# Agent attention and soft MoE on one core: the last product with its slots normalised ahead and its output written transposed

## The chip, the core and the metric

One core of one Trainium2 chip. The metric is the device time of one execution in microseconds, the median of several runs. The engines are TensorE (PE, with its weight loads PEld), VectorE (DVE), ScalarE (ACT), GpSimd (POOL) and SyncE (SP), which issues nearly all transfers here.

## The reference

Two layers in a row, all in float32. The first is an attention through 49 agents per batch, the second a mixture of experts over 32 slots:

```python
a2k = sm(agents, k)                 # (4, 49, 11456)
agent_v = a2k @ v                   # (4, 49, 128)
q2a = sm(q, agents)                 # (4, 11456, 49)
x = (q2a @ agent_v).reshape(45824, 128)

logits = x @ phi                    # (45824, 32 slots)
d = softmax(logits, over tokens)
slot_input = d.T @ x                # 32 x 128, four slots for each of 8 experts
slot_out[e] = relu(slot_input[e] @ w1[e]) @ w2[e]
c = exp(logits - logits.max(1))     # softmax over the slots
c /= c.sum(1) + 1e-9
return c @ slot_out                 # (45824, 128)
```

The softmax over tokens needs every token's logits before the experts can run, and the last product needs the experts' slot outputs.

## The kernel before

A cell is 128 tokens: 32 from each of four streams of a batch. A batch has 90 cells, the four batches 360. Cells are handled in groups of 16 (the last of a batch has 10). For each group of keys the kernel makes scores, a running maximum, exponentials, transposes and the weighted sum of v; for each group of queries it makes scores, the softmax over the agents, the logits of the slots (`lt`), their maximum per slot for the rounds of the token softmax, and their maximum per token.

The main part is written out as steps in one list, `ORDER`. A step's name is a family with an index (`qs.0`, `ke.1`), and steps of one family follow each other in the order of their groups. Each engine runs its own steps in list order. `BUFS` gives the number of buffers of each kind of tile.

The steps that matter here are those of the combine weights c. `cr` (DVE, L551) takes the row maximum `rm` of a group's logits, `cu` (POOL, L555) subtracts it into a buffer `xc`, `ce` (ACT, L561) takes the exponential, and `ct` (DVE, L565) transposes 32x32 blocks of it into `c_all`, the weights of all cells with the slots on partitions. For one group (`CT_PE`) the transpose is made by PE and ACT (`cp`, `cq`). The weights are left unnormalised.

The end of the list holds the last rounds of the token softmax (`r1` to `r5` for the maxima; `ru`, `re`, `rm`, `rg` for dt, its exponential, its product with `rt` and the sum on PE), then the merging of the rounds into the slot inputs `si`, the reciprocal `dr` of the token sums, the experts (`mh`, `mr` with tile `hs`, `mt` with tile `htp`, `mc` with tile `ht`, `mo`), their copies `so` and the product `sb`, which repeats the 32 slot outputs over four groups of 32 partitions. `fl` are matmuls without use, which keep PE running.

Then comes the output stage. Four cells make a quad, 90 quads in all. `c_split` (DVE L1043, POOL L1044) splits six quads of `c_all` into a high and a low part in a reduced float32 format (fp32r). `bd_hi` (L1058) and `bd_lo` (L1062) are the same for the slot outputs times `dr`, as block-diagonal matrices of two blocks, each block with a column of ones for the row sums. For a quad, PE makes three products (high by high, low by high, high by low) for two halves: six matmuls of 258 columns (L1079). DVE adds EPS to the row sums and takes the reciprocals (L1086, L1088); for each pair of quads DVE evicts the first with the reciprocals multiplied in (L1099), ACT the second in four pieces (L1103). Outputs go out in 17 batches of one to three pairs, with two transfers each, tokens on partitions.

Of the kernel before, what the change touches and what calls it, by code (L numbers as in the profile page):

```python
# [16 lines left out]
S = E * SE  # L17
P = 128
# [4 lines left out]
NQUAD = B * NCELL // 4  # L23
FULL = NCELL // 4 * 4
# [25 lines left out]
qx qx qs.0 qs.1 qx qt.0 qs.0 qt.1 qm kx qs.1 qE.0 qt.0 qE.1 qs.0 qt.1 kv qm qs.1 qE.2 qt.0  # L50
qp.0 qu ks.0 qE.3 qt.1 ks.1 kx qm qe qp.1 km.0 qc.0 qp.0 qw@0 km.1 qc.1 qp.1 qc.0 qr kt qw@1
qE.0 kv kr qr ks.0 qE.1 kb ks.1 km.0 kn ke.0 kx qp.0 km.1 ke.1 kP.0 qE.2 kt kr kb kT.0 kn ka
kP.1 kx qE.3 ks.0 kT.1 ke.0 ks.1 km.0 ke.1 kT.0 qp.1 kv qc.1 km.1 qw@2 qc.0 kE kT.1 qc.1 qr kx
kt ks.0 kA kr kb kE km.0 kn ka ke.0 ke.1 kT.0 kv kT.1 ks.1 kA ks.0 km.1 kt kE km.0 kx kr kb kv
ks.1 kA kn ka ke.0 km.1 ke.1 ks.0 kT.0 kt ks.1 kr kT.1 kx kb kn km.0 ka kE ke.0 km.1 ke.1 kT.0
kT.1 kt kv kr kE kA qx kb ks.0 kA kn ka ke.0 ks.1 ke.1 km.0 kT.0 km.1 kv kT.1 kt qs.0 kr kb kE
qt.0 kn ke.0 kx ke.1 kT.0 qs.1 kA kT.1 kg.2 qt.1 kg.1 kE kh.1 kh.2 qm kh.4 kv qu kg.3 kA ks.0
kh.3 ks.1 km.0 qe qx ql.0 km.1 ql.1 qn.0 kt ql.0 qn.1 kr qg ql.1 qn.0 kb kx qp.0 qn.1 kn ka qM
qp.1 ke.0 qg qs.0 cr ke.1 qM cu qc.0 qs.1 qt.0 qc.1 ql.0 ce r1 kv qt.1 ql.1 qn.0 qm ks.0 kT.0
r2 qE.0 ks.1 km.0 qx ql.0 kT.1 qE.1 km.1 ql.1 qn.0 r3 kx qE.2 ct kE cr qw@3 cu qE.3 kt qs.0 kA  # L60
kr ce qx qp.0 qt.0 rx kb qs.1 ct qc.0 kn ks.0 qr ka qt.1 ke.0 qn.1 qm r4 ke.1 qg qp.1 kT.0 r5
# [36 lines left out]
qu qc.1 ql.1 qn.0 r5 ru.0 qe cr ql.0 w1 qn.1 ql.1 ru.1 re.0 qn.0 ql.0 qM rm.0 re.1 qn.1 ql.1
rm.1 r1 qM w2 r2 rg.0 cu r3 qn.0 rx rg.1 r4 cr rc qp.0 ce qn.1 qp.0 r5 cu qc.0 en@12 cr qc.0
qp.1 w2 ru.0 qM ce qp.1 ql.0 qc.1 en@13 r1 en@14 qc.1 r2 ru.1 re.0 ql.1 qn.0 r3 ql.0 qn.1 rx  # L100
rm.0 re.1 w2 en@19 r4 qM ql.1 r5 fl rm.1 rg.0 qn.0 fl r1 cr ru.0 r2 rg.1 cr fl rc qn.1 fl w1
ru.1 en@15 re.0 r3 qM rx cr en@16 r4 rm.0 re.1 r1 ct en@17 r5 ct en@18 r2 fl rm.1 rg.0 r3 nm
rx wt fl ru.0 r4 f0 rg.1 r5 wr fl rc ws fl ru.0 re.0 f1 fl f2 fl rm.0 fl cu re.0 fl fl rm.0
rg.0 cu ce rg.0 rc gl fl cu fl l0 ce ct gm l1 fl cp l2 d0 cu ce l3 d1 l4 fl ct d2 mh ct ce ct
mh mr mh mr mt mt mc mr mh mc mt mr mo mc mt zz mo mc mo ms mo sb ms fl sb fl fl fl fl fl fl
fl
"""
BUFS = {
    "kt": 2, "vt": 3, "qt": 3, "es": 1, "et": 2, "pt": 8, "pT": 3, "lt": 5, "xc": 3, "dt": 2,
    "s": 4, "a": 3, "m": 1, "hs": 2, "ht": 3,  # L110
}
SUB_DVE = ()
MUL_DVE = (11, 12)
CT_PE = (21,)
# [1089 lines left out]
```

## Time and profile before

| | |
|---|---|
| median of 3 runs | 343.92 us (343.78 to 346.8) |
| the profiled execution | 343.8 us, its span as well; nothing lies around it |
| PE, DVE, ACT, POOL busy | 306.9, 283.7, 216.8, 145.6 us |
| read from and written to HBM | 79.98 MB, 23.59 MB |
| keys and queries up to the last maxima | 0 to about 244 us |
| last rounds, slot inputs, experts | 244 to 267.6 us |
| output stage | 267.66 us to the end |

A row of a view has the start or a count, the busy time, the engine, the line of the kernel and the tiles written and read; the time in brackets is how long the engine stood idle before it, with what ended that. Busy time of an engine in an average over the span says little here, since the three stretches differ; the rows by stretch and the chain of work that ended last are to be read together.

### The profile page before, as it was taken

The numbers are of one execution on the slowest core, as the hardware profiler recorded it, in microseconds if no ns is written. First come the engines' busy times: TensorE is split into PE (matmuls) and PEld (weight loads), VectorE is DVE, ScalarE is ACT, GpSimd is POOL, SyncE is SP. The second block draws the span as 40 slices with busy tenths as digits, with TensorE's granted clock in tenths as the row PEclk, the third lists the DMA queues.
The fourth block names the chain that finished last, engine by engine and source line by source line (L and its number), as shares of the span: only waits on it lengthen the run. The fifth ranks groups of instructions, "written<-read, shape, count | busy, mean of one in ns | idle before, by whom it ended". The sixth has DMA issues, their size and how long they took to land.

```text
span 343.8 us, 10606 instructions
## 1 busy us (share of the span) xinstructions
PE 306.9 (89%) x4177; PEld 207.9 (60%) x4177; DVE 283.7 (83%) x686; ACT 216.8 (63%) x773; POOL 145.6 (42%) x157
## 2 busy tenths in 40 slices
PE   2979979988988988898999999998989999999991
PEld 0235446554553554445655646487756999999990
DVE  0855755999999899999999999999894788888872
ACT  1597323494968586668776984555442577777772
POOL 0100001319371636447147937797955133444400
PEclk9999998999999999999999999999999999999996
DMA  7999899999889369989659961998000278888887
GB/s 302 423 407 363 287 409 425 418 396 379 334 322 369 126 225 418 352 309 382 270 218 396 378 272 19 394 421 350 2 2 4 92 286 357 359 342 343 336 348 295
DMA packets 16897, 104.25 MB, mean 303 GB/s; under 512 B 2000, under 2 KB 2128, under 8 KB 8144
## 3 DMA queue, kind: packets, MB, share of 16 engines
q1 hardware_dynamic: 16416, 102.95, 75.3%
q8 instruction: 33, 0.54, 0.6%
q10 hardware_dynamic: 432, 0.63, 0.5%
q14 instruction: 16, 0.13, 0.1%
HBM read 79.98 MB, written 23.59 MB: 301 GB/s over the span
## 4 chain that ended last, share of the span: by engine, by line
PE 42%; DVE 40%; ACT 6%; DMA 5%; issue 2%; POOL 1%; SPq 0%; ACTq 0%; DVEq 0%; POOLq 0%
PE po L1079 19%; DVE pt L444 6%; DVE cm L546 5%; PE sk L241 5%; PE ev L329 4%; DVE mx L449 4%; DVE et L311 4%; DVE kmx L273 3%; ACT pt L470 3%; DVE rm L551 3%; PE sq L241 3%; DMA qt<-qT 3%; DMA cs<-cst 3%; DVE row L285 3%; DVE lt L500 2%
## 5 line engine op out<-in xcount | busy, mean ns | idle before, releaser
L1103 ACT ACTIVATE ot<-po,rc 128x128 f32<-128x128 f32 x180 | 51.3, 368 | 19.3 <-DVE rc L1088 18.5
L470 ACT ACTIVATE pt<-pt,mx 128x49 f32<-128x49 f32 x160 | 51.4, 328 | 10.4 <-DVE mx L449 10.3
L241 PE MATMUL sq<-qt,ag 128*32 128x512 f32 (+1 forms) x384 | 48.0, 597 | 7.8 <-ACT ag L170 6.7
L329 PE MATMUL ev<-vt,et 128*64 128x129 f32 x720 | 46.4, 280 | 4.1 <-issue 1.4
L241 PE MATMUL sk<-kt,ag 128*32 128x512 f32 (+1 forms) x384 | 46.9, 573 | 1.4 <-DVE pt L444 1.0
L329 PEld LDWEIGHTS ev<-vt,et 128*64 128x64 f32 x720 | 40.2, 138 | 11.6 <-issue 4.9
L1044 POOL TENSOR_TENSOR cl<-c_all,ch 128x768 fp32r<-128x768 f32 x15 | 28.1, 1876 | 44.7 <-DVE rc L1086 38.6
L454 POOL TENSOR_TENSOR pt<-pt,mx 128x784 f32<-128x784 f32 (+1 forms) x14 | 19.3, 1378 | 57.2 <-DVE mx L449 56.3
L1079 PE MATMUL po<-bd_hi,ch 128*128 128x258 f32 x180 | 38.4, 295 | 0.2
L273 DVE TENSOR_REDUCE kmx<-sk 128x1 f32<-128x512 f32 (+1 forms) x48 | 30.6, 638 | 8.2 <-PE sk L241 7.9
L555 POOL TENSOR_TENSOR xc<-lt,rm 128x512 f32<-128x512 f32 (+1 forms) x24 | 24.5, 1024 | 28.4 <-DVE rm L551 22.9
L1079 PE MATMUL po<-bd_lo,ch 128*128 128x258 f32 x180 | 36.3, 283 | 0.0
L1079 PE MATMUL po<-bd_hi,cl 128*128 128x258 f32 x180 | 36.2, 282 | 0.0
L444 DVE STREAM_TRANSPOSE pt<-sq 128x512 f32<-128x512 f32 (+1 forms) x48 | 31.2, 659 | 2.2 <-PE sq L241 1.9
L1099 DVE TENSOR_TENSOR ot<-po,rc 128x512 f32<-128x512 f32 x45 | 31.1, 691 | 1.7 <-DVE rc L1088 0.2
L681 POOL TENSOR_TENSOR dt<-lt,mb 128x512 f32<-128x512 f32 (+1 forms) x24 | 28.6, 1209 | 8.1 <-ACT mb L675 7.4
L521 ACT COPY pT<-tp 128x512 f32<-128x512 f32 (+1 forms) x48 | 25.3, 556 | 9.9 <-PE tp L514 9.6
L311 DVE STREAM_TRANSPOSE et<-es 128x512 f32<-128x512 f32 (+1 forms) x46 | 29.8, 650 | 1.5 <-ACT es L300 1.5
L470 ACT ACTIVATION_READ_ACCUMULATOR pt<-pt,mx 128x1 f32 x160 | 30.6, 191 | 0.0
L300 ACT ACTIVATE es<-sk,nm 128x512 f32<-128x512 f32 (+1 forms) x48 | 29.3, 649 | 0.2
L505 POOL TENSOR_TENSOR lt<-lt,rt 128x512 f32<-128x512 f32 (+1 forms) x19 | 19.0, 999 | 23.4 <-DVE lt L500 23.3
L1079 PEld LDWEIGHTS po<-bd_hi,ch 128*128 128x128 f32 x180 | 27.6, 189 | 2.2 <-ACT bd_hi L1058 0.4
(134 smaller groups left out, 570.1 us busy)
## 6 DMA issues: line engine op xcount, KB each, us to landing
vt<-vL SPq DMA_DIRECT2D x20, 1032.0 KB, 9.5
qt<-qT SPq DMA_DIRECT2D x20, 1024.0 KB, 8.3
kt<-kT SPq DMA_DIRECT2D x20, 1024.0 KB, 7.0
out<-ot SPq DMA_DIRECT2D x26, 768.0 KB, 4.8
w1s<-w SPq DMA_DIRECT2D x4, 1024.0 KB, 9.9
w2s<-w SPq DMA_DIRECT2D x4, 1024.0 KB, 11.3
vt<-vL SPq DMA_DIRECT2D x4, 645.0 KB, 8.3
kt<-kT SPq DMA_DIRECT2D x4, 640.0 KB, 7.4
```

The lines of the kernel that those rows point to most:

```text
L241: t_.matmul(sp[32 * q4:32 * q4 + 32, :nt], ag[:, b, 32 * h:32 * h + 32], xv[:, q4, :], start=True, stop=True)
L273: v_.tensor_reduce(out=k["mx"][:, h:h + 1], in_=k["s"][h][:, :nt], axis=AX.X, op=ALU.max)
L300: s_.activation(out=k["e"][:, h, :nt], in_=k["s"][h][:, :nt], func=AF.Exp, bias=k["nm"][:, h:h + 1])
L311: v_.transpose(out=k["et"][:, :n, 32 * h:32 * h + 32], in_=k["e"][:, h, :nt].rearrange("p (t a) -> p t a", a=32))
L329: t_.matmul(k["ev"][o:o + 64, :], k["et"][:, c, :], k["v"][:, c, :], start=c < 2, stop=c >= n - 2)
L444: v_.transpose(out=q["pt"][:, :n, 32 * h:32 * h + 32], in_=q["s"][h][:, :nt].rearrange("p (t a) -> p t a", a=32))
L470: s_.activation(out=x, in_=x, func=AF.Exp, bias=q["mx"][:, c:c + 1], accum_out=q["dn"][:, c:c + 1])
L681: eng.tensor_tensor(out=q["dt"][:, :n], in0=q["lt"][:, :n, :], op=ALU.subtract, in1=r["mb"].unsqueeze(1).to_broadcast([P, n, S]))
L1044: nc.gpsimd.tensor_tensor(out=cl[:, :n], in0=src, in1=ch[:, :n].bitcast(F32), op=ALU.subtract)
L1079: t_.matmul(po[:, hf, 0:2 * VC], lh[:, i, :], rh[hf], start=ti == 0, stop=ti == 2)
L1099: v_.tensor_tensor(out=ov[0], in0=pos[2 * j][:, :, :, 0:C], in1=rc[:, 0].unsqueeze(3).to_broadcast([P, 2, 2, C]), op=ALU.mult)
L1103: s_.activation(out=ov[1][:, ha, hb], in_=pos[2 * j + 1][:, ha, hb, 0:C], func=AF.Copy, scale=rc[:, 1, ha, hb:hb + 1])
```

## The change

The combine weights now stay with the tokens on partitions: `cu` and `ce` write straight into `x_all`, which takes the place of `c_all`, and `xc`, `ct`, `cp`, `cq` and `c_split` are gone. The 360 cells are cut into 24 chunks (8, 21 times 16, 8, 8). For each chunk DVE takes the row sums, adds EPS and takes the reciprocals (`o_sum`, step `os`), POOL multiplies the weights by them (`o_mul`, step `om`), and DVE transposes the chunk into one of four `ct` buffers (`o_tr`, step `ot`). Six chunks are summed and multiplied, and four transposed, inside the list ahead of the output stage; the others inside the stage's loop, three chunks and one chunk ahead.

In the product the roles of the operands change: the slot outputs times `dr` (`sob`, one ACT activation, step `sd`) are the stationary operand and the weights the moving one, in plain float32. The 32 slots of each of the four streams stand in their own 32 partitions, so a chunk takes four matmuls with 32 contraction rows each, on four different row groups of PE, into four banks of PSUM. The result has the 128 channels on partitions. DVE copies one bank, ACT three, with no scaling, and one transfer takes the chunk out; the host puts the transposed output into its place.

```diff
-CT_PE = (21,)
-CG = 6
-OUT_SIZES = [1, 2] + [3] * 13 + [2, 1]
+CHUNKS = [8] + [16] * 21 + [8, 8]
+C0 = [sum(CHUNKS[:j]) for j in range(len(CHUNKS))]
+NORM = 6
+EARLY = 4
...
         def cu():
-            q["xc"] = tile_("xc", [P, QC, S], f"xc_{i}")
-            nc.gpsimd.tensor_tensor(out=q["xc"][:, :n, :], in0=q["lt"][:, :n, :],
+            nc.gpsimd.tensor_tensor(out=x_all[:, at:at + n], in0=q["lt"][:, :n, :],
...
-        def ct():
-            for c, m, o_ in c_spans(b, g):
-                v_.transpose(out=c_all[:, o_ * S:(o_ + m) * S],
-                             in_=q["xc"][:, c:c + m, :].rearrange("p c s -> p (c s)"))
...
+    def m_dr():
+        s_.activation(out=z["sob"], in_=z["sb"], func=AF.Copy, scale=dr)
+
+    def o_sum(j):
+        x = x_all[:, C0[j]:C0[j] + CHUNKS[j]]
+        z["cd", j] = wl(f"cd_{j}", [P, CHUNKS[j]], tag="cd", bufs=NORM)
+        v_.tensor_reduce(out=z["cd", j], in_=x, axis=AX.X, op=ALU.add)
+        v_.tensor_scalar(out=z["cd", j], in0=z["cd", j], scalar1=EPS, scalar2=None, op0=ALU.add)
+        v_.reciprocal(out=z["cd", j], in_=z["cd", j])
+
+    def o_mul(j):
+        n = CHUNKS[j]
+        x = x_all[:, C0[j]:C0[j] + n]
+        nc.gpsimd.tensor_tensor(out=x, in0=x, op=ALU.mult,
+                                in1=z["cd", j].unsqueeze(2).to_broadcast([P, n, S]))
+
+    def o_tr(j):
+        n = CHUNKS[j]
+        z["ct", j] = z["ct"][j % BUFS["ct"]]
+        v_.transpose(out=z["ct", j][:, :n * S],
+                     in_=x_all[:, C0[j]:C0[j] + n].rearrange("p c s -> p (c s)"))
...
-        for ti, (lh, rh) in enumerate([(ch, bd_hi), (cl, bd_hi), (ch, bd_lo)]):
-            for hf in range(2):
-                t_.matmul(po[:, hf, 0:2 * VC], lh[:, i, :], rh[hf],
-                          start=ti == 0, stop=ti == 2)
...
+    op_ = ctx.enter_context(tc.tile_pool(name="op", bufs=4, reuse_waits="tile"))
+    psO = ctx.enter_context(tc.tile_pool(name="psO", bufs=2, space=PSUM, reuse_waits="tile"))
...
+        for j, n in enumerate(CHUNKS):
+            if NORM <= j + 3 < len(CHUNKS):
+                o_sum(j + 3)
+                o_mul(j + 3)
+            if EARLY <= j + 1 < len(CHUNKS):
+                o_tr(j + 1)
+            po = psO.tile([P, 4, 512], F32, name=f"po_{j}", tag="o")
+            for r in range(4):
+                t_.matmul(po[:, r, :32 * n], z["sob"][32 * r:32 * r + 32, :],
+                          z["ct", j][32 * r:32 * r + 32, :32 * n], start=True, stop=True)
+            ot = op_.tile([P, 4 * 512], F32, name=f"ot_{j}", tag="ot")
+            ov = ot[:, :128 * n].rearrange("p (r x) -> p r x", r=4)
+            v_.tensor_copy(out=ov[:, 0], in_=po[:, 0, :32 * n])
+            s_.copy(out=ov[:, 1:4], in_=po[:, 1:4, :32 * n])
+            nc.sync.dma_start(out=out[:, 128 * C0[j]:128 * (C0[j] + n)], in_=ot[:, :128 * n])
```

In the list `ORDER` every `ct` is left out and `os`, `om`, `ot` and `sd` are put in near its end; the other steps keep their order. Three places show what that does on an engine. In the rows, a line number is that of the kernel the row belongs to, the tile written stands left of the arrow, and the shape is partitions by columns.

DVE where the last maxima of the queries are done (`rm` and `m_all`). Before:

```order
L551 TENSOR_REDUCE rm_3742<-lt_3680 128x10
L565 STREAM_TRANSPOSE c_all<-xc_3544 128x512
L565 STREAM_TRANSPOSE c_all<-xc_3585 128x512
L663 TENSOR_REDUCE m_all<-t_12_3758 32x1
L780 TENSOR_REDUCE nmx<-m_all 32x1
```

After:

```order
L541 TENSOR_REDUCE rm_3694<-lt_3632 128x10
L875 TENSOR_REDUCE cd_3701<-x_all 128x8
L876 TENSOR_SCALAR cd_3701<-cd_3701 128x8
L877 RECIPROCAL cd_3701<-cd_3701 128x8
L875 TENSOR_REDUCE cd_3712<-x_all 128x16
L876 TENSOR_SCALAR cd_3712<-cd_3712 128x16
L877 RECIPROCAL cd_3712<-cd_3712 128x16
L622 TENSOR_REDUCE m_all<-t_12_3718 32x1
L732 TENSOR_REDUCE nmx<-m_all 32x1
```

Two transposes gave their place to the row sums of the first two chunks.

POOL at the same time, among the last rounds' dt tiles (L651 is the product with `rt`, L640 the subtraction of the next rounds). After:

```order
L651 TENSOR_TENSOR dt_3642<-dt_3642,rt_3451 128x512
L882 TENSOR_TENSOR x_all<-x_all,cd_3701 128x256
L882 TENSOR_TENSOR x_all<-x_all,cd_3712 128x512
L651 TENSOR_TENSOR dt_3676<-dt_3676,rt_3501 128x512
L640 TENSOR_TENSOR dt_3749<-lt_3582,mb_3710 128x512
L640 TENSOR_TENSOR dt_3782<-lt_3632,mb_3770 128x320
```

Before, the two products stood next to each other; now two multiplications of combine weights stand between them.

DVE in the experts (`hs`, `ht`, `so`). Before:

```order
L857 TENSOR_TENSOR si<-si_p,sie 128x8x4
L870 TENSOR_SCALAR dr<-d_p 128x1
L871 RECIPROCAL dr<-dr 128x1
L565 STREAM_TRANSPOSE c_all<-xc_3884 128x512
L565 STREAM_TRANSPOSE c_all<-xc_3908 128x256
L565 STREAM_TRANSPOSE c_all<-xc_3908 128x64
L882 TENSOR_SCALAR hs_3936<-hp_3922 128x512
L1043 CAST ch_4005<-c_all 128x768
L1043 CAST ch_4009<-c_all 128x768
L1043 CAST ch_4119<-c_all 128x768
L882 TENSOR_SCALAR hs_3957<-hp_3938 128x512
```

After (one of three row sums between `si` and the first `hs` shown, and then from the `hs` on):

```order
L809 TENSOR_TENSOR si<-si_p,sie 128x8x4
L875 TENSOR_REDUCE cd_3874<-x_all 128x16
L876 TENSOR_SCALAR cd_3874<-cd_3874 128x16
L877 RECIPROCAL cd_3874<-cd_3874 128x16
...
L834 TENSOR_SCALAR hs_3902<-hp_3881 128x512
L834 TENSOR_SCALAR hs_3923<-hp_3904 128x512
L849 COPY ht_3930<-htp_3916 128x512
L849 COPY ht_3984<-htp_3958 128x512
L888 STREAM_TRANSPOSE ct_3255<-x_all 128x256
L888 STREAM_TRANSPOSE ct_3256<-x_all 128x512
L862 COPY so<-so_p_3939 128x128
```

The casts between the two `hs` are gone, more stands ahead of the first, and transposes stand ahead of the copies `so`.

More of the change, by code (lines that the diff above doesn't have):

```diff
@@ L56 @@
[L56 to L61, printed above, removed]
@@ L180, in tile_agent_attn_soft_moe @@
     sel_on = cs[0:S, CO_ON:CO_ON + P]
-    c_all = keep.tile([P, B * NCELL * S], F32, name="c_all")
+    x_all = keep.tile([P, B * NCELL, S], F32, name="x_all")
     g_all = keep.tile([P, NR, A1], F32, name="g_all")
@@ L767, in z_ms @@
         z["so"] = wl("so", [P, 2, C])
-        z["hi"] = [z["wp"].tile([P, 2, VC], F32R, name=f"bd_hi{h}") for h in range(2)]
-        z["lo"] = [z["wp"].tile([P, 2, VC], F32R, name=f"bd_lo{h}") for h in range(2)]
-        for h in range(2):
-            hi = z["hi"][h].bitcast(F32)
-            nc.gpsimd.memset(hi, 0.0)
-            nc.gpsimd.memset(z["lo"][h].bitcast(F32), 0.0)
-            for i in range(2):
-                r4 = slice(64 * h + 32 * i, 64 * h + 32 * i + 32)
-                nc.gpsimd.memset(hi[r4, i, C:VC], 1.0)
+        z["sob"] = wl("sob", [P, C])
+        z["ct"] = [wl(f"ct{x}", [P, 16 * S]) for x in range(BUFS["ct"])]
     def z_nm(e):
@@ L912, in m_sb @@
     def m_sb(eh):
-        for h in range(2):
-            if eh == 0:
-                z["sb", h] = tile_("a", [P, C], f"sb_p{h}")
-            t_.matmul(z["sb", h][64 * h:64 * h + 64], sel_h[eh][:, 64 * h:64 * h + 64],
-                      z["so"][:, eh, :], start=eh == 0, stop=eh == 1)
+        if eh == 0:
+            z["sb"] = tile_("a", [P, C], "sb_p")
+        t_.matmul(z["sb"], sel_h[eh], z["so"][:, eh, :], start=eh == 0, stop=eh == 1)
+    def m_dr():
[16 more added lines that the diff above has]
+                     in_=x_all[:, C0[j]:C0[j] + n].rearrange("p c s -> p (c s)"))
     def z_fl(n):
@@ L1065, in tile_agent_attn_soft_moe @@
-    ps.close()
-    psO = ctx.enter_context(tc.tile_pool(name="psO", bufs=4, space=PSUM, reuse_waits="tile"))
-    where = []
-    for n in OUT_SIZES:
-        where += [(len(where), i, n) for i in range(n)]
-    pos, ots = {}, {}
-    def o_mm(g):
-        po = psO.tile([P, 2, 512], F32, name=f"po_{g}", tag="o")
-        ch, cl = chs[g // CG]
-        i = g % CG
-        for ti, (lh, rh) in enumerate([(ch, bd_hi), (cl, bd_hi), (ch, bd_lo)]):
-            for hf in range(2):
-                t_.matmul(po[:, hf, 0:2 * VC], lh[:, i, :], rh[hf],
-                          start=ti == 0, stop=ti == 2)
-        pos[g] = po[:, :, 0:2 * VC].rearrange("p a (b c) -> p a b c", c=VC)
```

238 lines of the change are left out of this document (76 added, 162 removed).

## The prediction

> **What bounds the kernel now.** I read the page first, for the engines' shares and the chain that ended last, and then cut the span into stages, since a mean over stages with different limits says little.
>
> ```profile
> PE 306.9 (89%) x4177; PEld 207.9 (60%) x4177; DVE 283.7 (83%) x686; ACT 216.8 (63%) x773; POOL 145.6 (42%) x157
> HBM read 79.98 MB, written 23.59 MB: 301 GB/s over the span
> PE 42%; DVE 40%; ACT 6%; DMA 5%; issue 2%; POOL 1%; SPq 0%; ACTq 0%; DVEq 0%; POOLq 0%
> 60.00:80.00 20.00, 17.86 (x293) 10.04 (x285) 19.61 (x40) 13.12 (x50) 6.98 (x9) 1.00 1.00 408
> 80.00:205.00 125.00, 115.07 (x1910) 65.26 (x1910) 121.06 (x253) 93.41 (x366) 67.62 (x77) 1.00 0.81 318
> 205.00:244.00 39.00, 36.98 (x576) 27.24 (x569) 38.14 (x99) 21.26 (x51) 31.06 (x41) 1.00 0.65 261
> 244.00:267.60 23.60, 21.68 (x371) 15.25 (x371) 16.84 (x34) 9.20 (x23) 13.91 (x11) 1.00 0.01 2
> 267.60:338.00 70.40, 68.46 (x540) 66.55 (x540) 55.69 (x194) 51.33 (x180) 22.12 (x12) 1.00 0.79 317
> ```
>
> The chain is PE and DVE in almost equal parts. The rows by stage (length, then busy time of PE, weight loads, DVE, ACT and POOL, clock, DMA share, GB/s) say where each holds. From 80 to 244 us DVE is busy 159.2 of 164 us, with PE close behind (152.1): these two share the bound. From 244 to 267.6 a thin serial chain runs (last rounds, experts), and DMA is empty. From 267.6 us the product with the combine weights runs, and PE has no gap:
>
> ```profile
> 267.66 50.30 PE po L1079 x396
> 321.01 15.21 PE po L1079 x120
> 270.53 3.83 SPq L1107 DMA_DIRECT2D out<-ot  x4
> 335.85 3.65 SPq L1107 DMA_DIRECT2D out<-ot  x4
> out<-ot SPq DMA_DIRECT2D x4, 256.0 KB, 3.3
> ```
>
> These are the last pieces of the chain, the first and last output issues, and what a 256 KB output takes from issue to landing. 396 matmuls in 50.30 us are 0.127 us each; all 540 make 68.6 us. DMA stands at 0.79 beside it: the output stage is PE's, and DMA has room.
>
> **The change, term 1: the output stage.** The 540 matmuls and the per-quad reciprocals go. Instead every chunk of 16 cells gets four matmuls of 512 columns with 32 contraction rows each, one DVE eviction of 512 columns, one ACT eviction of 1536, and a 1.05 MB output. DVE also gets a chunk's row sums, their reciprocals and the transpose, POOL the multiplication. There are 22.5 full chunks' worth (360 cells by 16).
>
> ```profile
> 34.59 1.85 PE sk L241 x16
> 265.83 1.69 PE fl L922 x14
> L521 ACT COPY pT<-tp 128x512 f32<-128x512 f32 (+1 forms) x48 | 25.3, 556 | 9.9 <-PE tp L514 9.6
> L460 ACT ACTIVATE pt<-pt 128x784 f32<-128x784 f32 (+1 forms) x14 | 11.2, 801 | 6.3 <-POOL pt L454 6.0 <-POOL pt L456 0.3
> L551 DVE TENSOR_REDUCE rm<-lt 128x16 f32<-128x512 f32 (+1 forms) x24 | 15.0, 627 | 0.2 <-POOL lt L505 0.2
> L480 DVE TENSOR_SCALAR pt<-pt 128x16 f32<-128x16 f32 (+1 forms) x9 | 3.1, 339 | 0.3
> L484 DVE RECIPROCAL rt<-pt 128x16 f32<-128x16 f32 (+1 forms) x19 | 3.9, 212 | 0.9 <-POOL pt L474 0.9
> L444 DVE STREAM_TRANSPOSE pt<-sq 128x512 f32<-128x512 f32 (+1 forms) x48 | 31.2, 659 | 2.2 <-PE sq L241 1.9
> L897 DVE COPY ht<-htp 128x512 f32<-128x512 f32 x2 | 1.4, 682 | 1.8 <-PE htp L889 1.8
> L555 POOL TENSOR_TENSOR xc<-lt,rm 128x512 f32<-128x512 f32 (+1 forms) x24 | 24.5, 1024 | 28.4 <-DVE rm L551 22.9
> ```
>
> PE: no row shows matmuls side by side on different contraction rows. The nearest are the scores, four matmuls of 512 columns side by side on different output columns, in two passes each: 16 records, two such groups, in 1.85 us, 0.93 us a group. If row tiles run side by side the same way, a chunk costs 0.93 us. If they run in turn it costs 4 x 0.93 = 3.7 us. I take the near row, 0.93, and keep 3.7 as a rival.
>
> The Trainium skill, "TensorE: Matmul & The Clock Gate", section "Part 3: Packing small matmuls — row/col tiling", gives 3.07 times for four row tiles of 32 rows and 512 columns. By that rule a chunk would be an estimated 3.7 / 3.07 = 1.2 us, and the sum below would not move; nothing in this trace tests it.
>
> ACT: from 512 to 784 columns it takes 245 ns more, 0.90 ns a column; 1536 columns are 0.556 + 1024 x 0.0009 = 1.48 us. The ACT eviction waits for DVE's of the same chunk, and PE for ACT's of two chunks before, so a pair of chunks goes round in no less than 0.93 + 0.68 + 1.48 and some waits, about 1.7 us a chunk. DVE: 0.63 + 0.34 + 0.21 + 0.66 + 0.68 = 2.52 us. POOL: 1.02 us. DMA: 23.59 MB at the 408 GB/s of the full stretch are 57.8 us, 2.57 a chunk. So DMA becomes the bound, with DVE 0.05 us under it: a thin cover, though the rows overlap by some 0.06 us where neither waits for the other.
>
> The stage starts where it did: seven fillers (14 transposes, 1.69 us) still stand before its first matmul, and the one scaling that replaces the four bd_hi activations and the four bd_lo operations ends under them. From 267.66: 0.6 us of matmuls for the first half chunk, 0.4 DVE, 0.8 ACT, so the first output is issued at 269.5 (270.5 before). The second chunk's comes 2.2 us later, after the first's bytes are out: 0.9 us of gap. To land, 256 KB took 3.3 us, 0.8 of them at the stage's 317 GB/s, so 2.5 us are latency; 335.85 + 3.65 + 3.3 = 342.8 leaves 1.0 us to the end of the span. So 269.5 + 57.8 + 0.9 + 2.5 + 1.0 = 331.7 us: **12.1 us less** than the profiled 343.8. Bounds: latency and gap wholly hidden, 328.3; DVE's pace instead of DMA's, below.
>
> **Term 2: the transposes leave the main stage.**
>
> ```profile
> 88.81 0.59 DVE c_all L565
> 216.65 0.48 DVE c_all L565 x2
> L565 DVE STREAM_TRANSPOSE c_all<-xc 128x512 f32<-128x512 f32 (+2 forms) x27 | 14.8, 566 | 0.0
> ```
>
> 27 transposes go, 14.8 us; 21 of them before 244 us. The six from 244 us on take 1.28 + 0.70 + 1.14 = 3.1 us by the rows below, so 11.7 us leave the stretch in which DVE is the fuller engine. Of the 21 only eight pieces (the first and last of them above, each 0.48 to 0.66 us) lie on the chain, 4.8 us together. The stretches between run over PE, which is busy 115.07 of 125 us and whose instructions there stay. Bounds: 0 (PE takes the chain at once) and 11.7 (DVE alone sets the pace). I take the chain's **4.8 us less**. POOL's subtraction also stops waiting for a free xc buffer; it is never shown waiting for one, so nothing for that.
>
> **Term 3: the tail before the output gets longer.** Six row sums, six multiplications and four transposes move ahead of the experts' end.
>
> ```profile
> 244.00 1.28 DVE L565 STREAM_TRANSPOSE c_all<-xc 128x512 f32<-128x512 f32 x2
> 245.22 0.24 DVE L663 TENSOR_REDUCE m_all<-t 32x1 f32<-32x128 f32 x1
> 243.38 2.06 POOL L692 TENSOR_TENSOR dt<-dt,rt 128x512 f32<-128x512 f32 x2
> 245.88 2.10 POOL L681 TENSOR_TENSOR dt<-lt,mb 128x512 f32<-128x512 f32 x2 [0.45 <-ACT mrep L667]
> 246.08 1.10 DVE L828 TENSOR_SCALAR fd<-cs,wt 32x32 f32<-32x32 f32 x1 [0.44 <-ACT wt L788]
> 248.19 2.60 DVE L692 TENSOR_TENSOR dt<-dt,rt 128x512 f32<-128x512 f32 x2
> 251.97 0.70 DVE L565 STREAM_TRANSPOSE c_all<-xc 128x512 f32<-128x512 f32 x1
> 253.72 0.19 DVE L857 TENSOR_TENSOR si<-si_p,sie 128x32 f32<-128x32 f32 x1 [0.17 <-PE si_p L854]
> 254.31 1.14 DVE L565 STREAM_TRANSPOSE c_all<-xc 128x512 f32<-128x512 f32 x3
> 255.38 0.65 DVE L882 TENSOR_SCALAR hs<-hp 128x512 f32<-128x512 f32 x1
> 255.95 3.11 DVE L1043 CAST ch<-c_all 128x768 fp32r<-128x768 f32 x3
> 256.92 1.09 PE L889 MATMUL htp<-cs,hs 128*128 128x128 f32 x8
> 259.71 0.66 PE L889 MATMUL htp<-cs,hs 128*128 128x128 f32 x4 [0.71 <-DVE hs L882]
> 264.79 0.29 DVE L910 COPY so<-so_p 128x128 f32<-128x128 f32 x1 [1.46 <-PE so_p L905]
> ```
>
> One row sum is 0.63 + 0.34 + 0.21 = 1.18 us, the half one 0.87. (a) At 244.0 two of them, 2.05 us, take the place of 1.22; POOL's second new multiplication waits for the second, to 246.05, ends at 247.1, and the old dt multiplication queued behind it ends at 248.1 (245.4 before). The dt subtraction then starts at 248.1, not 245.88; 1.05 us of it and 0.6 of ACT's exponential later DVE's dt starts at 249.8, not 248.2: 1.6 us. (b) At 251.97: 1.18 for 0.70, 0.5 us, and the copy behind it feeds si. (c) After si, three row sums (3.54) and dr (0.35) stand before the first hs, 3.9 us against 1.5 now, 2.4 late. But the three casts between the two hs go, so the second follows at once. PE's first eight transposes, at 256.92 now, would start when the first hs ends, at 258.4, 1.5 us late; the next four, which stood 0.7 us for the second hs, do not stand: 0.8 us late. (d) At the so copies four transposes stand on DVE, two of them ahead of the last so: 0.5 us. Together **3.4 us more**. Bounds: each new tensor_scalar may be held as long as L828, 1.10 us, which ran beside POOL's subtraction: six times 0.76 make 8.0. Below, 1.5, if the slack that PE shows at (a) takes its part.
>
> **Sum:** 331.7 - 4.8 + 3.4 = 330.3 us. The profiled execution took 343.8, the median of the three runs 343.92, so the same holds for the median.
>
> **The rivals.** A, the row tiles do not overlap, so the change does not do what its name says: 22.5 x 3.7 = 83.3 us of PE from 267.66, to 351.0, then 0.4 + 0.8 for evictions, 3.8 for the last 0.5 MB to land (2.5 latency + 1.3) and 1.0: 357.0, less 1.4 of terms 2 and 3, 355.6, slower. It decides for slower from 3.18 us a chunk (267.66 + 22.5 x 3.18 + 6.0 - 1.4 = 343.8). For it: no row tiling in this trace. Against it: the scores' 0.93, and PE could lose two thirds of the overlap before it passes DMA's 2.57.
>
> B, evictions and DVE's own work bound: if the tensor_scalar is held by POOL in every chunk (1.10 for 0.34, as in L828), DVE needs 3.28 us. Three chunks at ACT's pace to 273, 18 at 3.28 are 59, the last three 2.5, ACT 0.8, landing 3.8, end 1.0: 340.1 - 1.4 = 338.7. It decides from 2.57 us. For it: the 0.05 us of cover. Against: POOL's 1.02 us multiplication starts after the sum that it reads, and has 1.3 us of transpose and copy to run beside before the next tensor_scalar. The Trainium skill, "TensorEngine Tiling (Array Packing)", section "PSUM Bottleneck", warns that tiling does not speed up the way out of PSUM; if that holds here the time is B's; in the rows above ACT's 1.48 us stay under DMA's 2.57.
>
> C, DVE alone set the main stage's pace: 331.7 - 11.7 + 1.5 = 321.5. Against: PE at 92%.
>
> D, within the forecast's own range, nothing from the main stage and a tail held everywhere: 331.7 + 8.0 = 339.7.
>
> **How the numbers follow.** Forecast with its bounds (325 to 340) 0.66, C 0.11, B 0.12, A 0.11. The range must leave out no more than 0.2: from 321 to 341 it leaves out A and a little of B and C. What a measurement of this kernel tells from no change is about 1%, 340.5 to 347.4: faster 0.82 (forecast, C, most of B), same 0.07, slower 0.11.
>
> **What would show it.** Term 1: po groups of 8 records in about 1 us, DMA share near 1.0 and 400 GB/s from 273 us on, gaps on DVE released by DMA. A: eight records of a chunk starting one after another. B: DMA under 0.9 and tensor_scalar rows over 0.5 us. Term 2: main-stage events (last weights' issue, the g_all scaling) about 5 us earlier. Term 3: the stretch from the last m_all to the first output matmul over 22.4 us by some 3. The forecast is wrong if DMA writes rows of 8 KB well below the 408 GB/s of the loads, since the 57.8 us are its largest term.

## The result, and the profile after

The changed kernel takes 335.79 us (median of four runs, 333.75 to 341.17) against 343.85 for the kernel before: a ratio of 0.9709, 95% interval 0.9639 to 0.9780. In the experiments' first set it was 0.9638 (0.9591 to 0.9684), with a median of 335.73. The prediction was 330.3: right in direction and within its range, but 5.5 us short of the median.

A part of that is bookkeeping. In every later run, of either kernel, the time is 1.7 to 2.0 us above the span of the core. The table before called both 343.8; an execution with that span should take an estimated 345.6. The prediction's sum is therefore one of spans: 330.3 stands beside the 332.0 of the profiled execution, whose time is 333.75. Spans are compared below. The two spans differ by 11.8 us, while the medians differ by 8.1 us here and by 12.6 in the experiments' first set (348.36 to 335.73): the gain itself is known to a few microseconds only. Executions of the changed kernel differ by 0.8% (mean clock granted to PE 0.921 to 0.934 in those compared here), so differences under 3 us are read from traces, not from times; but a trace is one execution too, and where the times of all executions say otherwise, the text says so. Two profiled executions among the experiments, named there, were much longer than the others of their kernel, and no stretch of theirs is compared.

From the page: busy time, bytes, and the chain that ended last.

```profile
PE 274.5 (83%) x3821; PEld 152.7 (46%) x3821; DVE 264.7 (80%) x580; ACT 195.7 (59%) x613; POOL 139.8 (42%) x158
HBM read 79.98 MB, written 23.59 MB: 312 GB/s over the span
DVE 44%; PE 29%; DMA 11%; ACT 7%; POOL 4%; issue 3%; SPq 0%; ACTq 0%; DVEq 0%; POOLq 0%
```

PE has lost 32 us of work and 13 points of the chain; DMA has gone from 5% to 11% of it. By stage (length, busy time of PE, weight loads, DVE, ACT, POOL, mean of PE's granted clock as a share of full speed, DMA share, GB/s):

```profile
80.00:205.00 125.00, 116.75 (x1974) 66.74 (x1970) 116.54 (x245) 94.97 (x371) 69.99 (x79) 1.00 0.80 316
205.00:244.00 39.00, 35.69 (x529) 26.05 (x528) 37.72 (x95) 19.26 (x48) 27.41 (x32) 1.00 0.65 261
244.00:269.10 25.10, 21.64 (x320) 15.58 (x321) 14.89 (x35) 6.79 (x16) 12.12 (x12) 0.87 0.01 2
269.10:327.00 57.90, 35.45 (x192) 10.36 (x192) 43.40 (x98) 32.62 (x24) 18.00 (x18) 0.72 0.95 394
```

In the main stage PE, with 116.75 of 125 us, now stands level with DVE (before 115.07 and 121.06). In the output stage PE is busy for 35 of 58 us, at a mean clock of 0.72 (it stands at 1.0 or at 0.5, called half clock below), and DMA's share goes from 0.79 to 0.95. Rows of the chain in that stage, the output transfers and the DVE copies:

```profile
269.12 0.75 PE po L1025 x8
271.20 1.18 PE po L1025 x8
281.59 2.10 PE po L1025 x8
302.96 1.45 ACT ot L1030
304.42 8.12 DMA out<-ot
out<-ot SPq DMA_DIRECT2D x21, 1024.0 KB, 6.8
L1029 DVE COPY ot<-po 128x512 f32<-128x512 f32 (+1 forms) x24 | 15.4, 643 | 12.6 <-DMA out<-ot 7.7
```

A chunk's eight records take 1.18 us at full clock and 2.10 at half. DVE's copy stands 7.7 us for output buffers that DMA has not yet emptied, so DMA sets the pace; the run with half of the output, below, tests this. Cut at the first output matmul and at the m_all of the round before the last, the spans differ so:

| stretch | before | after | difference | forecast |
|---|---|---|---|---|
| up to that m_all | 242.79 | 240.49 | -2.3 | -4.8 |
| from there to the first output matmul | 24.87 | 28.63 | +3.8 | +3.4 |
| from the first output matmul to the end | 76.1 | 62.9 | -13.2 | -12.1 |
| span | 343.8 | 332.0 | -11.8 | -13.5 |

### The profile page after: what moved, and what is told of

It reads as the page before. It is cut to its first block, busy times and chain, and to the rows that moved or that the text cites. A ratio compares the mean times of both kernels' runs of the same rounds, so it can differ in the third digit from the quotient of the medians.

```text
span 332.0 us, 9455 instructions
## 1 busy us (share of the span) xinstructions
PE 274.5 (83%) x3821; PEld 152.7 (46%) x3821; DVE 264.7 (80%) x580; ACT 195.7 (59%) x613; POOL 139.8 (42%) x158
## 3 DMA queue, kind: packets, MB, share of 16 engines
HBM read 79.98 MB, written 23.59 MB: 312 GB/s over the span
## 4 chain that ended last, share of the span: by engine, by line
DVE 44%; PE 29%; DMA 11%; ACT 7%; POOL 4%; issue 3%; SPq 0%; ACTq 0%; DVEq 0%; POOLq 0%
PE ev L318 5%; DVE cm L536 5%; DMA out<-ot 5%; DVE pt L434 5%; PE sk L230 5%; PE sq L230 4%; ACT pt L460 3%; DVE mx L439 3%; DVE kmx L262 3%; DVE et L300 3%; DVE rm L541 3%; PE po L1025 3%; DMA qt<-qT 3%; DMA cs<-cst 3%; DVE row L274 3%
## 5 line engine op out<-in xcount | busy, mean ns | idle before, releaser
L460 ACT ACTIVATE pt<-pt,mx 128x49 f32<-128x49 f32 x160 | 51.4, 328 | 10.6 <-DVE mx L439 10.5
L1025 PE MATMUL po<-ct,sob 32*128 32x512 f32 (+1 forms) x192 | 35.4, 819 | 17.9 <-DVE ct L888 13.0
L318 PE MATMUL ev<-vt,et 128*64 128x129 f32 x720 | 45.1, 276 | 3.3 <-DVE lt L490 1.4
L1030 ACT COPY ot<-po 128x1536 f32<-128x1536 f32 (+1 forms) x24 | 32.6, 1359 | 24.5 <-DVE ot L1029 24.5
L318 PEld LDWEIGHTS ev<-vt,et 128*64 128x64 f32 x720 | 39.3, 136 | 10.6 <-issue 2.3
L882 POOL TENSOR_TENSOR x_all<-x_all,cd 128x512 f32<-128x512 f32 (+1 forms) x24 | 23.9, 994 | 41.6 <-DVE cd L877 38.7
L544 POOL TENSOR_TENSOR x_all<-lt,rm 128x512 f32<-128x512 f32 (+1 forms) x24 | 24.2, 1015 | 25.3 <-DVE rm L541 21.4
L640 POOL TENSOR_TENSOR dt<-lt,mb 128x512 f32<-128x512 f32 (+1 forms) x24 | 28.7, 1212 | 7.4 <-ACT mb L634 7.1
L1025 PEld LDWEIGHTS po<-ct,sob 32*128 32x128 f32 x192 | 10.4, 240 | 42.5 <-ACT ot L1030 42.2
L504 PE MATMUL tp<-cs,pt 128*128 128x128 f32 x180 | 27.2, 282 | 0.7 <-ACT pt L450 0.5
L504 PEld LDWEIGHTS tp<-cs,pt 128*128 128x128 f32 x180 | 19.3, 141 | 14.4 <-issue 4.2
L1029 DVE COPY ot<-po 128x512 f32<-128x512 f32 (+1 forms) x24 | 15.4, 643 | 12.6 <-DMA out<-ot 7.7
```

What stands on the lines that cost most here:

```text
L318: t_.matmul(k["ev"][o:o + 64, :], k["et"][:, c, :], k["v"][:, c, :], start=c < 2, stop=c >= n - 2)
L460: s_.activation(out=x, in_=x, func=AF.Exp, bias=q["mx"][:, c:c + 1], accum_out=q["dn"][:, c:c + 1])
L504: t_.transpose(q["tp", h][:, (c - h0) // 2, :], q["pt"][:, c:c + 2, :].rearrange("p c a -> p (c a)"), ident)
L640: eng.tensor_tensor(out=q["dt"][:, :n], in0=q["lt"][:, :n, :], op=ALU.subtract, in1=r["mb"].unsqueeze(1).to_broadcast([P, n, S]))
L1025: t_.matmul(po[:, r, :32 * n], z["sob"][32 * r:32 * r + 32, :], z["ct", j][32 * r:32 * r + 32, :32 * n], start=True, stop=True)
L1030: s_.copy(out=ov[:, 1:4], in_=po[:, 1:4, :32 * n])
```

## The experiments

Each kernel is the changed one with the edit shown. Ratios are against the kernel before on the same chip and in the same set.

**The base once more.** 

> The changed kernel once more, unchanged, as the base for the three kernels below. 335.8 us give or take 1.5: the four runs so far went from 333.8 to 336.3 with the granted clock (0.934 down to 0.926 over the span), since PE falls to half clock in windows of some 7 us late in the span. If the clock is what moves the time, a run with a higher mean clock is the shorter one again.

335.73 us, span 334.2 in its trace. The stretches after the main stage repeat: 28.95 and 62.94 us. The main stage was 1.9 us longer: 2.7 us were lost by 58 us, in two half-clock windows (25.7 to 29.1 and 53.0 to 56.4) that the first trace does not have, and 0.8 won back near 195.

**The old transposes back in the main stage.**

```
-        o("ce", (), "A", 100 + 26 * n, ce, deps=(f,))
+        f = o("ce", (), "A", 100 + 26 * n, ce, deps=(f,))
+        if i < 18:
+            o("ct", (), "V", 70 + 33 * n, ct, deps=(f,))
```

> The changed kernel with the 18 old DVE transposes of the main stage (one for each group of cells, 0.57 us each, about 10.3 us of DVE) put back at their old places in the order; they write into a scratch tile that nothing reads. Theory (term 2: only the pieces on the chain count): 3.0 to 4.8 us slower than the changed kernel, main-stage events later by as much at 200 us. Rival (PE takes the chain at once): within 1 us. Rival (DVE alone sets the pace of the main stage): 9 to 10 us slower. If the 1.3 us by which the changed kernel led already at 60 us came from a half-clock window of the old run, ct_back keeps that part, and its loss is nearer 3.

340.57 us, ratio 0.9695 (0.9620 to 0.9770), which overlaps the base's 0.9591 to 0.9684: the time does not decide. The trace says more. Four rounds' m_all on DVE, first before, then after, then three of them with the transposes back (start, duration):

```profile
71.53 0.24 DVE L663 TENSOR_REDUCE m_all<-t 32x1 f32<-32x128 f32 x1
178.67 0.27 DVE L663 TENSOR_REDUCE m_all<-t 32x1 f32<-32x128 f32 x1
222.63 0.24 DVE L663 TENSOR_REDUCE m_all<-t 32x1 f32<-32x128 f32 x1
242.79 0.28 DVE L663 TENSOR_REDUCE m_all<-t 32x1 f32<-32x128 f32 x1
```

```profile
70.25 0.24 DVE L622 TENSOR_REDUCE m_all<-t 32x1 f32<-32x128 f32 x1
174.38 0.27 DVE L622 TENSOR_REDUCE m_all<-t 32x1 f32<-32x128 f32 x1
219.47 0.24 DVE L622 TENSOR_REDUCE m_all<-t 32x1 f32<-32x128 f32 x1
240.49 0.28 DVE L622 TENSOR_REDUCE m_all<-t 32x1 f32<-32x128 f32 x1
```

```profile
70.66 0.24 DVE L629 TENSOR_REDUCE m_all<-t 32x1 f32<-32x128 f32 x1
177.73 0.27 DVE L629 TENSOR_REDUCE m_all<-t 32x1 f32<-32x128 f32 x1
222.73 0.24 DVE L629 TENSOR_REDUCE m_all<-t 32x1 f32<-32x128 f32 x1
```

Between the first and the second of these rounds the transposes cost 177.73 - 174.38 - 0.41 = 2.9 us, and 222.73 - 219.47 - 0.41 = 2.9 still at the third; the lead of after over before grows by the same 3.0 between the first two (1.28 to 4.29). It comes in five steps of some 0.6 us, each one transpose that stood on the chain; the other thirteen, some 8 us of DVE time, cost nothing up to there. Term 2's mechanism holds, with 2.9 in place of 4.8. (From 234 to 248 us this trace has half clock, so nothing later is read from it.)

The first 1.3 us of the lead have nothing to do with the change: it is there before the first transpose that was removed. The same stretch, before and after:

```profile
51.40:54.90 3.50, 3.50 (x40) 2.42 (x36) 1.53 (x3) 1.44 (x3) 0.00 (x0) 0.51 1.01 425
```

```profile
51.40:54.90 3.50, 3.50 (x48) 1.85 (x40) 2.37 (x5) 1.44 (x3) 0.00 (x0) 1.00 1.00 423
```

The old trace had half clock here, with PE full, and the changed one had not. The base run again has such a window, and an earlier one too, and in place of the lead of 1.3 us it has a lag of 1.4.

**No row sums and no multiplications.** The steps `os` and `om` are left out of the list too.

```
-        f = op("os", (j,), "V", 800, lambda j=j: o_sum(j), deps=ends_ + [ms])
-        f = op("om", (j,), "G", 1000, lambda j=j: o_mul(j), deps=(f,))
...
-                o_sum(j + 3)
-                o_mul(j + 3)
```

> The changed kernel without row sums and multiplications (the weights are left unnormalised; the four transposes before the output stage stay). Theory (term 3: row sums on DVE and multiplications on POOL lengthen the tail): the stretch from the last weight round's m_all at 240.5 to the first output matmul falls from 28.6 to about 25.5 us, the time by some 3 us; the output stage keeps its 62 to 63 us, since DMA at 417 GB/s sets it and DVE's work there was hidden. Rival (the tail's half-clock window at 243.9 to 250.7, not the sums, makes it long): less than 1.2 us faster. Rival (DVE still counts in the output stage): that stage becomes shorter by more than 1.5 us too.

330.82 us, 0.9496 (0.9438 to 0.9553). In its trace the tail (the stretch from that m_all to the first output matmul) takes 26.23 us, 2.4 to 2.7 less; the output stage 62.7, unchanged. So by the traces the row sums cost 2.4 to 2.7 us, all of it by the six in the tail. The medians differ by twice as much, 4.9 us from the base, and what the other half is stays open.

**The row sums where DVE waits.**

```
-r1 os om en@17 r5 os om en@18 r2 fl ... f0 rg.1 ... fl cu fl l0 ce os om gm ... l4 fl os om d2 mh os om ce os om mh
+r1 en@17 r5 en@18 r2 fl ... f0 os os rg.1 ... fl cu om om fl l0 ce gm ... l4 fl os om d2 mh ce mh
-mr mh mr mt mt mc mr mh mc mt mr mo mc mt zz mo mc ot ot mo ms ot ot mo sb
+mr os om mh mr mt mt mc mr mh mc os om ot ot mt mr mo mc mt zz mo mc ot mo ms ot mo sb
-NORM = 6
+NORM = 5
```

> The changed kernel with the same work in another order: five row sums and multiplications ahead of the output stage in place of six, put where DVE waited (two behind the scaling of fd, one behind si, one between the two relu steps, one behind the ht copy), the first two multiplications on POOL behind the last dt work, and the transposes at the ht copies, only one ahead of the last so copy. Theory (term 3's parts a to d, each a place where a sum stands ahead of something that waits): 2.5 to 3.5 us faster than the changed kernel, tail stretch 25 to 26 us. Rival (PE or the half clock holds the tail, so the sums only fill): within 1 us.

333.66 us, 0.9559 (0.9498 to 0.9621). Its profiled execution took 831.61 us, so the tail is read from a second set of runs.

> The version with the row sums in other places, seven fillers and the old chunk sizes, once more, for its trace and its time beside the two kernels above. Expected: tail 24.0 us (the 22.9 of the version with one filler, plus 1.1), stage 62.9, 1.2 to 2 us over that version and 3 to 4 us under the changed kernel. If the tail takes 25.5 or more, PE's half clock has come back into it.

332.39 us, 0.9576 (0.9527 to 0.9625), tail 24.29, stage 62.76. Both intervals overlap the base's 0.9591 to 0.9684, so by the times a gain of 2 to 3 us is likely and not certain. In the trace the tail has lost 4.3 us against the changed kernel, more than leaving the sums out altogether did. The clock differs. From 240 to 252 us, after, without sums, and with the sums moved:

```profile
240.00:252.00 12.00, 10.07 (x167) 8.37 (x167) 7.21 (x21) 4.86 (x15) 10.31 (x10) 0.72 0.01 1
```

```profile
240.00:252.00 12.00, 12.00 (x184) 9.93 (x175) 6.81 (x17) 5.07 (x16) 9.89 (x10) 0.64 0.01 3
```

```profile
240.00:252.00 12.00, 9.64 (x206) 7.83 (x194) 9.17 (x24) 5.90 (x17) 11.55 (x12) 1.00 0.02 3
```

Without sums PE is busy for all of the 12 us, at 0.64 of its clock; with the sums moved it does more (206 matmuls to 184) in 9.64 us. The tail with no sums and half clock (26.23) is 1.9 us longer than the one with its sums and full clock (24.29). Nearly all of the 1.9 lies ahead of si, which starts 13.24 us behind that m_all without sums, 11.40 with the sums moved, 10.93 before the change and 14.08 after it; from si on, the two need 13.0 and 12.9 us, the changed kernel 14.6. So of the 3.8 us by which the changed kernel's tail grew, the sums' 2.4 to 2.7 are measured; that the rest is a half-clock window from 243.85 to 250.67, which the old trace does not have, is argued from these traces, since no run changes the clock alone. Why the clock fell here is not shown; it fell somewhere between 234 and 255 us in all eight traces compared that keep the sums at their first places or leave them out, and in neither of the two with the sums moved. That does not make full clock a merit of the new places: this profiled execution has the highest mean clock of its set (0.943, the others 0.925 and 0.926) and the shortest time, and by the times of all executions leaving the sums out (0.9496) is faster than moving them.

**Seven fillers more in the tail.**

```
-r1 os om en@17 r5 os om en@18 r2 fl rm.1 rg.0 r3 nm rx wt fl ru.0 r4 f0
+r1 os om en@17 fl r5 os om en@18 fl r2 fl rm.1 rg.0 r3 nm rx wt fl fl fl ru.0 r4 fl fl fl f0
```

> The changed kernel with seven more fillers (of two 128x128 transposes each) at the places where its PE stood in the tail: one behind each of the last two en steps, one more behind the transposes of the last weight round, two behind wt and three behind the last m_all transposes, ahead of the gp that waits for POOL. Theory (the changed kernel's tail has two parts, the row sums in the way and PE's half clock from 243.9 to 250.7, and the second is worth about 2 us: a tail without any row sum but with that window took 26.2 us, one with the sums elsewhere and no such window 22.9, of which 1.1 are fillers): the clock stays at 1.0 there and the tail takes 26.5 to 27.5 us in place of 28.6 to 29.0. Rival (half clock there costs nothing, the wait for POOL's dt is what ends last): 28.6 to 29.5, the clock whatever it is.

334.66 us, 0.9640 (0.9581 to 0.9698): no difference from the base can be told. The mean clock of the executions compared was a little higher (0.933 to 0.944, the base 0.921 to 0.930) and their times a little lower (332.3 to 335.8, the base 334.3 to 336.1), which leans to the theory; but its profiled execution was the longest of the four, 339.54 us, and its tail is not compared. The clock stood at 0.5 there from 238.68 to 252.33 us, so in that execution the fillers did not keep it up; the experiment does not decide what the half clock costs.

**The output matmuls in turn.**

```
-            for r in range(4):
-                t_.matmul(po[:, r, :32 * n], z["sob"][32 * r:32 * r + 32, :],
-                          z["ct", j][32 * r:32 * r + 32, :32 * n], start=True, stop=True)
+            for r in range(4):
+                t_.matmul(po[:, r, :32 * n], z["sob"][:, r], z["ct", j][:, :32 * n],
+                          start=True, stop=True)
```

> The changed kernel with the output's four matmuls of a chunk each over all 128 rows, the scaled slot outputs copied by four small ACT operations into four stationary tiles that are zero outside their 32 rows: same output, nothing side by side. Theory (rival A's price, and the reason that it did not happen): a chunk costs 4 x 0.93 = 3.7 us on PE at full clock, the stage 22.5 x 3.7 + 6 = 89 us in place of 62.9, the time some 360 us, about 25 over the changed kernel; PE is then full and its clock stays at 1.0. Rival (the overlap of the row tiles is not what pays, DMA or the evictions set the pace anyway): within 2 us of the changed kernel.

357.74 us, 1.0302 (1.0248 to 1.0355). The group of the output matmuls over the whole run, and 60 us of the stage:

```profile
L1028 PE MATMUL po<-ct,sob 128*128 128x512 f32 (+1 forms) x192 | 77.8, 567 | 0.7 <-ACT ot L1033 0.6
280.00:340.00 60.00, 60.00 (x142) 26.57 (x141) 39.90 (x90) 25.20 (x18) 17.37 (x17) 1.00 0.75 309
```

PE is full, at full clock, 77.8 / 22.5 = 3.46 us a chunk, and DMA falls back to 0.75. Rival A's mechanism is real; what kept it away is the overlap, 3.46 against 1.18 us, 2.9 times. The Trainium skill, "TensorE: Matmul & The Clock Gate", section "Part 3: Packing small matmuls — row/col tiling", gives 3.07 times; the estimate that the prediction worked out from it, 1.2 us a chunk, was nearer to the 1.18 than the 0.93 that it took from the scores.

**Two row tiles.**

```
+            for r in (0, 2, 1, 3):
+                k = slice(64 * (r // 2), 64 * (r // 2) + 64)
+                t_.matmul(po[:, r, :32 * n], z["sob"][k, r], z["ct", j][k, :32 * n],
+                          start=True, stop=True)
```

> The same with two row tiles of 64 rows, so two pairs of matmuls in turn, each pair side by side. Theory: 1.9 us a chunk on PE, still under DMA's 2.5, so the stage stays at 62 to 63 us and the time within 1 us of the changed kernel (335.5), though PE has lost half of the overlap; with PE at some 75% of the stage the half-clock windows there should become fewer, and that should bring nothing. Rival (half-clock windows cost time in the output stage): over 1.5 us faster. Rival (the two output buffers in PSUM tie PE, DVE and ACT into a round that DMA's pace does not cover): slower by 3 us or more.

337.73 us, 0.9710 (0.9659 to 0.9762), span 336.2: 2.0 over the base's second trace, where within 1 was forecast (the intervals overlap). One output group from its chain, and 40 us of the stage:

```profile
281.74 2.00 PE po L1029 x8
280.00:320.00 40.00, 33.88 (x138) 13.07 (x136) 36.99 (x85) 24.43 (x17) 16.93 (x17) 1.00 1.01 418
```

PE takes 2.00 us a chunk, DMA keeps its 418 GB/s, and the clock stays at 1.0 in these 40 us. The stage takes 64.1 us against 62.9: the 1.2 more are at its start, where the first chunks come later. Full clock brought nothing to a stage that DMA sets: the changed kernel moves 419 GB/s there at a mean clock of 0.75 (its row stands under the next run).

**Half of the output.**

```
-   nc.sync.dma_start(out=out[:, 128 * C0[j]:128 * (C0[j] + n)], in_=ot[:, :128 * n])
+   nc.sync.dma_start(out=out[:, 128 * C0[j]:128 * C0[j] + 64 * n], in_=ot[:, :64 * n])
```

> The changed kernel with only the first half of each chunk's output columns written (the rest of the output is left out), so DMA has 28 us of work in a stage of 63. It shows what stands next behind DMA. By the prediction's DVE term (2.52 us a chunk, 0.05 under DMA) the stage shrinks by 1 to 2 us only. By the rows of the changed kernel's trace (row sum 0.63, add 0.18, reciprocal 0.25, transpose 0.65, copy 0.65, fewer of them than chunks, some 48 us in all) it shrinks by 8 to 12 us, to 51 to 55, with DVE busy nine tenths of it. If the half clock of PE is next instead, DVE stays under eight tenths.

327.18 us, stage 53.1, 9.8 less. Thirty microseconds of the stage, with half of the output and with all of it:

```profile
280.00:310.00 30.00, 21.10 (x108) 6.12 (x112) 28.78 (x67) 18.70 (x13) 13.77 (x14) 0.77 0.55 227
```

```profile
280.00:310.00 30.00, 19.93 (x104) 5.33 (x96) 27.89 (x64) 18.53 (x13) 12.87 (x13) 0.75 1.01 419
```

DVE is next, 28.78 of 30 us, as forecast, but not at 2.52 us a chunk: the groups of this trace's chain follow each other every 2.29 us (284.32 to 298.04, six chunks). DMA's cover over DVE is 0.2 us a chunk, not 0.05. PE at half clock stands close behind: six of its chunks lie on this chain with 1.8 to 2.1 us each (2.04 for the one at 284.32), and DVE waits for them by no more than some 0.1 us.

**One held instruction taken off DVE.**

```
-            v_.tensor_scalar(out=k["rm"], in0=mask_ab, scalar1=ra, scalar2=None, op0=ALU.mult)
+            s_.activation(out=k["rm"], in_=mask_ab, func=AF.Copy, scale=ra)
```

> The changed kernel with the small tensor_scalar rm_a (128x2) put on ACT. In the changed kernel's trace it takes 1.39 us on DVE at 214.8, beside a POOL operation, and the lead over the old kernel falls by 1.1 us there. Theory (DVE is held while POOL runs, and this instruction lies on the chain): DVE's events from 217 to 230 us come 0.7 to 1.1 us earlier against the changed kernel than they do before 214, and the last weight round's m_all too. Rival (the next DVE instruction is held in its place, or DMA, at 1.01 from 217 us on, sets the pace): less than 0.3 us.

334.19 us, 0.9582 (0.9533 to 0.9631), which overlaps the base. The instruction and the POOL operation beside it, before and after:

```profile
219.03 0.23 DVE L359 TENSOR_SCALAR rm_a<-cs,ra 128x2 f32<-128x2 f32 x1
219.11 1.52 POOL L454 TENSOR_TENSOR pt<-pt,mx 128x784 f32<-128x784 f32 x1
```

```profile
214.78 1.39 DVE L348 TENSOR_SCALAR rm_a<-cs,ra 128x2 f32<-128x2 f32 x1
214.57 1.52 POOL L444 TENSOR_TENSOR pt<-pt,mx 128x784 f32<-128x784 f32 x1 [1.24 <-DVE ra L344]
```

Before, POOL was late by 1.7 us of bd_hi and bd_lo memsets, and rm_a slipped in ahead of its multiplication. The change removed the memsets, the multiplication came first, and rm_a ended only when POOL did (216.17 and 216.09). The Trainium skill, "SBUF — State Buffer", section "SBUF: two separate sides", states that of POOL and a DVE instruction that uses the ports which the two share (a tensor_scalar can be one), whichever starts first keeps them for its whole instruction. The rows agree: the order of the two starts decided. But taking the hold away won little. The next long PE group, after and with rm_a on ACT:

```profile
216.32 1.92 PE L230 MATMUL sq<-qt,ag 128*32 128x512 f32 x16
```

```profile
218.61 1.92 PE L230 MATMUL sq<-qt,ag 128*32 128x512 f32 x16
```

The second trace runs 2.29 us behind the first here, before the instruction as after it: PE did not start earlier, and DVE, freed of the hold, waited 0.47 us for PE. The last-but-one m_all came at 242.33, against 242.34 in the base's second trace, though 0.4 of lag at 200 us was made up. The theory falls: the hold is real, but at most 0.4 of its 1.16 us lay on the chain. Of the lead of 4.3 us at 178, 3.2 are left at 222 and 2.3 at 242; where most of that loss comes from stays open.

**A faster version.** The kernel with the row sums moved, with two edits more:

```
-FILL = (0, 4, 4, 3, 4, 3, 7)
-CHUNKS = [8] + [16] * 21 + [8, 8]
+FILL = (0, 4, 4, 3, 4, 3, 1)
+CHUNKS = [4, 8] + [16] * 21 + [8, 4]
```

> late_norm with two changes more: one filler in place of seven behind the last sb (the first output matmul stood 1.2 us behind the scaled slot outputs, for the fillers' sake alone), and the chunks' sizes 4, 8, 21 of 16, 8, 4 in place of 8, 21 of 16, 8, 8. Theory: 2 to 3 us from the row sums' places, 1.1 from the fillers, 0.5 to 0.8 from the first issue and the last landing: 4 to 5 us faster than the changed kernel, tail stretch 24 to 25 us, stage 62 to 62.5. Rival (with fewer fillers PE's clock falls as the stage begins and the first chunks come late): no more than 3 us faster.

332.12 us, 0.9521 (0.9469 to 0.9574); the interval lies under the changed kernel's 0.9591 to 0.9684, so it beats the kernel before and, by 1.2% or some 4 us, the changed one. From the version with the moved sums alone (0.9559 and 0.9576) it cannot be told apart. Tail 22.94, stage 63.4. What the fillers had cost, after and here:

```profile
267.28 1.69 PE L894 MATMUL fl<-cs 128*128 128x128 f32 x14
267.48 0.37 ACT L870 ACTIVATE sob<-sb_p,dr 128x128 f32<-128x128 f32 x1 [4.86 <-PE sb_p L867]
```

```profile
263.81 0.94 PE L1024 MATMUL po<-ct,sob 32*128 32x128 f32 x16 [0.24 <-ACT sob L869]
```

After, the scaled slot outputs were ready at 267.85 and the fillers ran until 268.97; here the first output matmul waits for ACT alone. The stage did not get shorter with the smaller first and last chunks; the two edits were not run apart.

## Why the prediction was right, and where it was off

**Term 1, the output stage: right, 1.1 us too small.** 62.9 us against a forecast 64.0. The bound moved to DMA as said, at 417 to 419 GB/s where the loads' 408 had been taken: 23.59 MB in 56.4 us, not 57.8. Row tiles overlap, at 1.18 us (0.93 forecast), with room to 2.0 shown. ACT's 1536 columns take 1.44 us (1.48 forecast). DVE's 2.52 us was too high by 0.2, most of it since the small tensor_scalar takes 0.18 us for the 0.34 of L480's row; in the stage none of them took longer, so B stayed away.

**Term 2, the main stage: the right mechanism, mis-sized.** "I take the chain's 4.8" counted eight pieces; five of them made a lead, 2.9 us. The one at 104.87 us made none: the lead stays at 2.5 us from 93 to 121 us, and PE's `tp`, `sq` and `sk` stand on the old chain from 108.14 us on. The prediction said that PE's instructions stay, but not that PE, at 115 of 125 us, swallows some of the pieces. It also missed that removing POOL's memsets moves POOL's multiplication ahead of a DVE instruction. Of the measured 2.3 us, 1.3 are a half-clock window of the old trace, which a comparison of two single executions cannot tell from the change: without it this stretch would have gained 1.0, not 4.8, since 2.0 of the lead are lost between 178 and 242 us, most of that for reasons that stay open.

**Term 3, the tail: right in sum, 3.8 against 3.4, partly for another reason.** The places were right. From the changed kernel's timeline, the dt multiplication behind POOL's second new one, si, one of the two adds that POOL held, the first hs, and PE's wait for it:

```profile
244.68 1.05 POOL L651 TENSOR_TENSOR dt<-dt,rt 128x512 f32<-128x512 f32 x1
254.57 0.18 DVE L809 TENSOR_TENSOR si<-si_p,sie 128x32 f32<-128x32 f32 x1
257.86 0.58 DVE L876 TENSOR_SCALAR cd<-cd 128x16 f32<-128x16 f32 x1
258.64 0.63 DVE L834 TENSOR_SCALAR hs<-hp 128x512 f32<-128x512 f32 x1
259.33 1.09 PE L841 MATMUL htp<-cs,hs 128*128 128x128 f32 x8 [1.25 <-DVE hs L834]
```

The multiplication ends 5.2 us behind the m_all of the round before the last, 2.6 before the change: 2.6 late, 2.7 forecast. The first hs starts 4.1 us behind si, 3.9 forecast. But the sums together cost 2.4 to 2.7 us by the traces, and without them the tail is still 1.4 us longer than before the change, with half clock in it. No term of the prediction has a half clock, so that 3.4 came out near 3.8 is in part luck. The fillers ahead of the first output matmul were taken over as a fixed 1.69 us, though sob was ready 1.1 us before their end.

**The rivals.** A did not happen; its price, 355.6, came out at a span of 355.0 when the matmuls were put in turn. B and C did not happen. D's long tail did not come: of the six tensor_scalars there only two took longer than 0.18 us, 0.32 and 0.58, and each of them ended with a POOL multiplication that had started before it.

## What to carry to other kernels

When a stage goes from one engine to DMA, what is left to win lies in what stands ahead of its first transfer: there sums and fillers in front of a waiting instruction count, and the same work in an engine's idle places can count nothing. A removed instruction is worth its time only where it stands on the chain, and only until the next engine is full. Before a difference of 1 or 2 us between two traces is given to a change, look for stretches of half clock in either.

## What the runs showed of the hardware

- Four row tiles of 32 rows and 512 float32 columns: 1.18 us a chunk against 3.46 for four full-height matmuls, and 2.00 for two pairs of 64 rows.
- PE's granted clock falls to 0.5 for 3.4 us or a multiple of it, at places that change from execution to execution (of the changed kernel's two traces one has no fall ahead of 243 us, the other has them at 26 and 53). In the stage that DMA sets this cost no throughput (419 GB/s at a mean clock of 0.75); at 51 us, with PE full, it cost 1.3 us.
- In the eleven traces compared, all changes of the clock lie on a grid of 3.41 us, which starts elsewhere in each execution. From 8 us on, and outside the stretch from 230 us to the first output matmul, each of the 43 falls follows a piece of the grid with PE busy for 18 to 54% of it, and of 753 pieces at full clock without a fall behind them all but 8 have 57% or more. From 230 us to the first output matmul the falls follow pieces with PE busy for 51 to 100%, so this does not explain those of the tail.
- A DVE instruction on 128x2 elements took 1.39 us in place of 0.23 when a POOL operation had started 0.21 us before it.
- Rows of 8 KB go out at 417 to 419 GB/s; the loads ran at 408 from 60 to 80 us before the change, and at 423 to 425 from 51.4 to 54.9.
